# The last 512 tokens of x turned by VectorE and carried by sixteen transfers, in a fused state-space and feed-forward kernel

## The chip, the cores and the metric

The kernel runs on one core of a Trainium2 chip. The metric is the device time of one execution in microseconds, as a median of several runs. The engines of a core are TensorE (PE, with its weight loads as PEld), VectorE (DVE), ScalarE (ACT), GpSimd (POOL) and SyncE (SP), which here only issues transfers.

## What is computed

One input x of 2048 tokens by 448 features goes two ways, and a gate for each token mixes the results.

```python
def _A_ref(x, Lambda_re, Lambda_im, B_re, B_im, C_re, C_im, log_dt, Dskip):
    ...
    Lam_bar = jnp.exp(dt * Lam)
    B_bar = ((Lam_bar - 1.0) / Lam)[:, None] * Bmat
    Bu = jnp.einsum("bld,pd->blp", x + 0j, B_bar)
    for t in range(L):
        h = Lam_bar[None, :] * h + Bu[:, t, :]
    ...
    y = 2.0 * jnp.einsum("blp,dp->bld", hseq, Cmat).real + x * Dskip[None, None, :]

def _B_ref(x, w1, w2):
    h = _silu(jnp.einsum("bsd,df->bsf", x, w1))
    return jnp.einsum("bsf,fd->bsd", h, w2)

g = _sigmoid((x * gate_w).sum(-1, keepdims=True))
return g * a + (1 - g) * b
```

The feed-forward width is 1792, the state has 448 complex channels, and everything that goes in or out is bf16.

## The kernel before

The 2048 tokens are cut into four chunks of 512 (`tc` 0 to 3). x is loaded with tokens in the partitions (`xnat`, `load_xn`, L423). The products need it with features in the partitions: `xT`, in four groups of 128 features that start at the columns `XCOL = [0, 128, 256, 320]`, the last two overlapping. For chunks 1 to 3 `x_transposes` (L498) has PE make 32 transposes of 64 by 64 against an identity (L508) into two PSUM banks, and two engines empty these into xT (L516 on DVE, L518 on ACT); for chunk 3 both evictions are ACT's.

`x_products` (L647) multiplies xT by w1 (tiles named F, 14 a chunk, emptied by ACT with the silu into `aT`) and by the state's input weights BT (tiles named B, 7 a chunk, emptied into `UG`: by DVE for chunk 0, by ACT for the others, L640 and L642). Each tile is a sum over seven products of 64 rows (L663), two tiles at a time in two PSUM banks.

`lanes` (L703 to L766) is DVE's large part, chunk by chunk: it turns UG by a phase (products with COS and SIN) into H, runs seven scans over 512 tokens (`tensor_tensor_scan`, L736) into Gf, and turns the result back into H. For chunks 0 to 2 POOL's queue carries each scan from Gf back to UG, cast to bf16 (L390 by way of L744); for chunk 3 ACT copies it. A chunk's scans start from the end of the chunk before (`gin`).

`ffn2` (G, L774) multiplies aT by w2. ACT empties it into one of two buffers `fe` (L780), scaled by the gate, and POOL's queue adds fe to xnat by an accumulating transfer (L782); the buffer may be filled again when that transfer has landed. xnat then holds g times the skip term, written by ACT at L849. `readout` (C, L795) multiplies H by the output weights CP, DVE adds xnat (L798), and SP stores the rows (L801). `gates` (L833) makes the gate: DVE's products xg and xnat (L704), ACT's sums (L842) and the tanh. `readout_weights` makes CP from C, with DVE's evictions at L827 and L830.

`H[3]` first holds the input weights B as they were loaded (`Bnat`, L411), then serves as chunk 3's H from `lanes(3)` on.

The order of the work comes from a planner (`Plan.order`, L104). PE takes its work in the order in which it was written; for the other engines the planner picks, at each point, the ready operation with the smallest priority number, by estimated durations and hops. PSUM banks are given out in the same pass. `Waits` (L204) then writes the engines' lists, with a semaphore wait wherever an operand is made or read elsewhere. So an added operation moves others on its engine, and the built program fixes the result. Loads by SP go first in its list; behind them it has only the stores.

Of the kernel before, what the change touches and what calls it, by code (L numbers as in the profile page):

```python
# [11 lines left out]
BF16 = DT.bfloat16  # L12
I32 = DT.int32

S_TOK = 2048
D_MOD = 448
F_FF = 1792
CH = 512
# [4 lines left out]
NOT = 5  # L23
NWARM = 6
NFILL = 2
XCOL = [0, 128, 256, 320]

TURN = 6.283184
# [248 lines left out]
def bass_gated_mix__ssm_conv_s5__dense_activation_silu__prompt_kernel(nc, A_x, A_Lambda_re, A_Lambda_im, A_B_re, A_B_im, A_C_re, A_C_im,  # L277
               A_log_dt, A_Dskip, B_x, B_w1, B_w2, gate_w, out):
    with ExitStack() as ctx:
# [6 lines left out]
        x2, out2 = A_x[0], out[0]  # L286

        xnat = sb("xnat", [128, NTB, D_MOD], BF16)
        xT = sb("xT", [128, 4, S_TOK], BF16)
        w1s = sb("w1s", [128, 4, F_FF], BF16)  # L290
        w2s = sb("w2s", [128, NFB, D_MOD], BF16)
        BT = sb("BT", [128, 4, 896], BF16)
# [175 lines left out]
        def x0_transposes(q0, part, who):  # L468

            tk = Ps(2)  # L470

            def mm(pe):
                for q in (q0, q0 + 1):
                    for k in range(2):
                        o = ((q - q0) * 2 + k) * 64
                        for h in range(2):
                            p = slice(64 * h, 64 * h + 64)
                            r = pe.transpose(bk(tk, h).bitcast(BF16)[:, o:o + 64], xnat[p, 2 * part + k, XCOL[q]:XCOL[q] + 128], ident[p, p])  # L478
                return r
            PE(mm, [f"xn0{part}", "ident"], [tk], 4 * 0.054, "xT0")  # L480
            for h in range(2):
                src = lambda h=h: bk(tk, h).bitcast(BF16)[:, 0:256].rearrange("p (q b n) -> p q b n", q=2, n=64)
                dst = xT[:, q0:q0 + 2, 256 * part:256 * part + 256].rearrange("p q (b h n) -> p q b h n", h=2, n=64)[:, :, :, h, :]
                names = [f"xT0_{q}{part}{h}" for q in (q0, q0 + 1)]
                if who[h] == "d":
                    DVE(lambda e, src=src, dst=dst: e.tensor_copy(dst, src()), [tk], names, 0.28, 0, "xTe")  # L486
                else:
                    ACT(lambda e, src=src, dst=dst: e.activation(dst, src(), AF.Copy), [tk], names, act_cost(256), 0, "xTe")
# [4 lines left out]
        x0_transposes(2, 1, "dd")  # L493

        xn_of = {tc: {q: [f"xT{tc}_{h}" for h in range(2)] for q in range(4)} for tc in range(1, NCH)}
        xn_of[0] = {q: [f"xT0_{q}{part}{h}" for part in range(2) for h in range(2)] for q in range(4)}

        def x_transposes(tc, who):  # L498

            tk = Ps(2)  # L500

            def mm(pe):
                for q in range(4):
                    for b in range(4):
                        o = (q * 4 + b) * 64
                        for h in range(2):
                            p = slice(64 * h, 64 * h + 64)
                            r = pe.transpose(bk(tk, h).bitcast(BF16)[:, o:o + 64],  # L508
                                             xnat[p, 4 * tc + b, XCOL[q]:XCOL[q] + 128], ident[p, p])
                return r  # L510
            PE(mm, [f"xn{tc}", "ident"], [tk], 16 * 0.035, f"xT{tc}")
            for h in range(2):
                src = lambda h=h: bk(tk, h).bitcast(BF16).rearrange("p (q b n) -> p q b n", q=4, b=4)
                dst = xT[:, :, tc * CH:(tc + 1) * CH].rearrange("p q (b h n) -> p q b h n", h=2, n=64)[:, :, :, h, :]
                if who[h] == "d":
                    DVE(lambda e, src=src, dst=dst: e.tensor_copy(dst, src()), [tk], [f"xT{tc}_{h}"], 0.69, 2.2, "xTe")  # L516
                else:
                    ACT(lambda e, src=src, dst=dst: e.activation(dst, src(), AF.Copy), [tk], [f"xT{tc}_{h}"], act_cost(1024), 2.2, "xTe")  # L518

        cosn = [f"COS{k}" for k in range(4)] + ["COSd"]  # L520
        sinn = [f"SIN{k}" for k in range(4)] + ["SINd"]
# [101 lines left out]
        def evict(pair, tk):  # L623

            kinds = [t[0] for t in pair]
            for k, n in ((0, 2),) if pair[0][:2] == pair[-1][:2] and len(pair) == 2 else ((0, 1), (1, 1))[:len(pair)]:
                kind, tc, a = pair[k]
                step = pair[k + 1][2] - a if n == 2 else 1
                sl = slice(a, a + step * (n - 1) + 1, step)
                names = [t[2] for t in pair[k:k + n]]  # L630
                src = (lambda: bk2(tk)) if n == 2 else (lambda k=k: bk(tk, k)[:, None, :])
                if kind == "F":
                    dst = aT[tc % 2][:, sl, :]
                    ACT(lambda e, src=src, dst=dst: e.activation(dst, src(), AF.Silu),  # L634
                        [tk, "tbl"], [f"aT{tc % 2}_{m}" for m in names], act_cost(512 * n), 2.5, "silu")
                    continue
                U, un = UG[tc % 2], f"U{tc % 2}_"
                dst = U[:, sl, :]
                if tc == 0:
                    DVE(lambda e, src=src, dst=dst: e.tensor_copy(dst, src()), [tk], [f"{un}{m}" for m in names], 0.15 + 0.53 * n, 2.6, "U")  # L640
                else:
                    ACT(lambda e, src=src, dst=dst: e.activation(dst, src(), AF.Copy), [tk], [f"{un}{m}" for m in names], act_cost(512 * n), 5, "U")  # L642
                if 3 in names:
                    load("pool", U[0:64, 7, :], U[64:128, 3, :], un + "7a", 65536, 9, [un + "3"])
                    load("pool", U[64:128, 7, :], U[0:64, 3, :], un + "7b", 65536, 9, [un + "3"])

        def x_products(tiles, fill={}, wait=()):  # L647

            part = (list(zip([(i, 64) for i in (0, 1, 2, 3)], [(i, 0) for i in (0, 1, 3, 2)])),
                    list(zip([(i, 0) for i in (0, 1, 2)], [(i, 64) for i in (0, 1, 3)])))
            pairs = [tiles[t:t + 2] for t in range(0, len(tiles), 2)]
            toks = [Ps(2) for _ in pairs]

            def steps(k, h, a, z):
                def body(pe):
                    for n, cut in list(enumerate(part[h]))[a:z]:  # L660
                        for b, ((i, p0), tile) in enumerate(zip(cut, pairs[k])):
                            tc = tile[1]
                            r = pe.matmul(bk(toks[k], b), weights(tile, p0, p0 + 64, i), xT[p0:p0 + 64, i, tc * CH:(tc + 1) * CH],  # L663
                                          start=(h == 0 and n == 0), stop=(h == 1 and n == 2))
                    return r
                reads = [n for cut in part[h][a:z] for (i, _), tile in zip(cut, pairs[k])
                         for n in xn_of[tile[1]][i] + (w1n(tile[2], i) if tile[0] == "F" else btn[tile[2]])]
                return PE(body, list(dict.fromkeys(reads)), [toks[k]], (z - a) * PE_MM[512], f"{pairs[k][0][0]}{pairs[k][0][1]}")

            def half(k, h):  # L670
                if h == 0 and pairs[k][0] == ("F", 0, 0):
                    def zero(pe):
                        for n in range(NFILL):
                            for b, p in enumerate((slice(64, 128), slice(0, 64))):
                                r = pe.matmul(bk(toks[k], b)[:, 0:128], ones[p, 0:128], ones[p, 0:128], start=True, stop=True)  # L675
                        return r
                    PE(zero, [], [toks[k]], NFILL * 0.11, "fill")
                    steps(k, 0, 0, 2)
                    steps(k, 0, 2, 4)
                else:  # L680
                    steps(k, h, 0, len(part[h])).own = h == 1
                if h:
                    evict(pairs[k], toks[k])

            half(0, 0)
            for f in fill.get(-1, ()):
                f()
            for k in range(len(pairs)):
                order = [lambda: half(k, 1)] + [lambda: half(k + 1, 0)] * (k + 1 < len(pairs))
                for n, f in enumerate(order if k - 1 in wait else order[::-1]):  # L690
                    f()
                    for m in fill.get((k, n), ()):
                        m()
                for f in fill.get(k, ()):
                    f()
# [173 lines left out]
        gates(0)  # L869
        gates(1)  # L870
        lanes(1)
        for f in cp(0) + G(0, 1) + cp(1, 2) + G(2, 3) + cp(3):
            f()
        x_products(F(1) + F(2, 0, 1) + B(2), {2: xt(2, "aa")})
        gates(2)
        lanes(2)
        for f in G(4, 5, 6, 7) + C(0, 1, 2, 3):
            f()
        x_products(F(2, 1) + B(3) + F(3), {1: xt(3, "aa"), 9: [lambda: gates(3), lambda: lanes(3)]})
        for f in C(4, 5, 6, 7) + G(8, 9, 10, 11):  # L880
            f()
        for f in C(8, 9, 10, 11) + G(12, 13, 14, 15) + C(12, 13, 14, 15):
# [36 lines left out]
```

## Time and profile before

| what | us |
|---|---|
| median of three runs | 141.94 |
| lowest and highest of them | 141.46, 142.53 |
| the profiled execution | 141.25 |
| its span, first to last instruction | 139.5 |
| busy in it: PE | 135.9 |
| DVE | 122.0 |
| ACT | 90.3 |
| POOL | 39.2 |
| chunk 3's transposes on PE (32, at 77.23) | 0.47 |
| chunk 3's evictions of xT on ACT (2, at 78.19) | 1.93 |

Times in the views are microseconds from the start of the span. The chain of work that ended last is followed back from the last instruction: at each step to what released it, or to the instruction before it on its engine. A timeline line gives start, length, engine, source line, operation, what is written from what, shapes, and in brackets the idle time before it with what ended it; neighbours of the same kind are merged (x2). For transfers, the time to landing runs from the issue to the semaphore.

### The profile page before, as it was taken

What the parts mean: (1) busy time and instruction counts of PE and PEld (TensorE: products, weight loads), DVE (VectorE), ACT (ScalarE), POOL (GpSimd) and SP (SyncE); (2) the same over time, 40 slices, a digit from 0 to 9 for tenths busy, and PEclk for the clock granted to TensorE, in tenths of its full rate; (3) what the DMA queues carried; (4) which work ended last, traced back from release to release, by engine and by line L of the source; (5) the groups of instructions that cost most, each with busy time, mean ns of one, the idle gap of its engine ahead of it and who ended that gap; (6) DMA issues with size and microseconds to landing.
All of it is one profiled execution on the core that took longest, in us unless ns stands there. A gap on an engine that the chain in (4) does not pass through costs nothing.

```text
span 139.5 us, 3000 instructions
## 1 busy us (share of the span) xinstructions
PE 135.9 (97%) x1201; PEld 67.0 (48%) x1201; DVE 122.0 (87%) x179; ACT 90.3 (65%) x157; POOL 39.2 (28%) x72
## 2 busy tenths in 40 slices
PE   7999999999999999999999999999999999999992
PEld 2445454455544544455544544444455555555561
DVE  0319999999999999999999999999999999997053
ACT  3349768999989999823694887799931268312300
POOL 7134040100248440227733001824000314022220
PEclk9999999999999999999999999999999999999999
DMA  4998999510156770104976200674202322323242
GB/s 136 337 294 243 363 320 238 177 42 0 31 79 94 129 110 1 38 15 73 157 131 155 38 5 0 95 133 79 38 4 97 66 33 36 83 83 61 40 94 71
DMA packets 17956, 14.71 MB, mean 105 GB/s; under 512 B 2835, under 2 KB 17814, under 8 KB 17942
## 3 DMA queue, kind: packets, MB, share of 16 engines
q0 software_dynamic: 6064, 5.51, 24.8%
q1 hardware_dynamic: 11318, 8.65, 20.7%
q10 hardware_dynamic: 560, 0.36, 0.8%
q8 instruction: 9, 0.15, 0.4%
q14 instruction: 5, 0.04, 0.1%
HBM read 7.17 MB, written 1.84 MB: 65 GB/s over the span
## 4 chain that ended last, share of the span: by engine, by line
PE 97%; DVE 0%; issue 0%
PE ps L663 46%; PE ps L774 31%; PE ps L795 15%; PE ps L463 2%; PE ps L508 1%; PE ps L478 1%; PE ps L814 1%; PE ps L604 1%; DVE ot L798 0%; PE ps L675 0%; PE ps L464 0%; PE ps L536 0%
## 5 line engine op out<-in xcount | busy, mean ns | idle before, releaser
L663 PE MATMUL ps<-xT,w1s 64*128 64x512 bf16 x392 | 48.5, 378 | 0.0
L774 PE MATMUL ps<-w2s,aT 128*128 128x448 bf16 x224 | 43.2, 353 | 0.0
L634 ACT ACTIVATE aT<-ps 128x1024 bf16<-128x1024 f32 (+1 forms) x30 | 28.7, 969 | 8.5 <-PE ps L663 8.4
L774 PEld LDWEIGHTS ps<-w2s,aT 128*128 128x128 bf16 x224 | 21.7, 98 | 20.4 <-ACT xnat L849 0.4
L663 PEld LDWEIGHTS ps<-xT,w1s 64*128 64x128 bf16 x392 | 19.7, 94 | 22.3 <-DVE xT L486 0.7
L663 PE MATMUL ps<-xT,BT 64*128 64x512 bf16 x196 | 25.8, 376 | 0.0
L782 POOL DMA_DIRECT2D xnat<-fe x16 | 14.1, 900 | 37.9 <-ACT fe L780 37.2
L780 ACT ACTIVATE fe<-ps,g 128x448 bf16<-128x448 f32 x16 | 10.1, 632 | 21.1 <-PE ps L774 21.0
L390 POOL DMA_DIRECT2D UG<-Gf x27 | 14.7, 549 | 20.9 <-DVE Gf L736 20.4
L736 DVE TENSOR_TENSOR_SCAN Gf<-rc,gin,H 128x512 f32<-128x512 f32 x14 | 17.2, 1268 | 0.0
L795 PE MATMUL ps<-CP,H 128*128 128x448 bf16 (+2 forms) x98 | 16.4, 326 | 0.0
L663 PEld LDWEIGHTS ps<-xT,BT 64*128 64x128 bf16 x196 | 10.8, 94 | 11.1 <-DVE Gf L562 0.2
L798 DVE SCALAR_TENSOR_TENSOR ot<-ps,g,xnat 128x448 bf16<-128x448 f32 (+2 forms) x18 | 10.8, 622 | 6.0 <-issue 4.6
L390 POOL DMA_DIRECT2D UG<-UG x8 | 4.8, 597 | 29.2 <-ACT UG L642 17.4
L704 DVE TENSOR_TENSOR H<-UG,COS 128x3584 bf16<-128x3584 bf16 (+4 forms) x10 | 12.6, 1266 | 0.0
L795 PEld LDWEIGHTS ps<-CP,H 128*128 128x128 bf16 x98 | 8.9, 98 | 7.5 <-DVE k L752 0.4
L642 ACT ACTIVATE UG<-ps 128x1024 bf16<-128x1024 f32 (+1 forms) x12 | 10.7, 923 | 1.4 <-PE ps L663 1.4
L842 ACT ACTIVATE junk<-xg 128x448 bf16<-128x448 bf16 x16 | 9.2, 574 | 2.1 <-DVE xg L704 2.0
L849 ACT ACTIVATE xnat<-xnat,g 128x448 bf16<-128x448 bf16 x16 | 9.8, 671 | 0.2
L704 DVE TENSOR_TENSOR PI<-UG,SIN 128x512 bf16<-128x512 bf16 (+2 forms) x13 | 9.1, 722 | 0.0
L704 DVE TENSOR_TENSOR PO<-UG,SIN 128x1536 bf16<-128x1536 bf16 (+1 forms) x8 | 8.7, 1087 | 0.1
L736 DVE TENSOR_TENSOR_SCAN Gf<-rc,gin,H2C 128x512 f32<-128x512 f32 x7 | 8.5, 1265 | 0.0
(102 smaller groups left out, 126.5 us busy)
## 6 DMA issues: line engine op xcount, KB each, us to landing
UG<-Gf POOLq DMA_DIRECT2D x21, 128.0 KB, 2.5
xnat<-fe POOLq DMA_DIRECT2D x16, 112.0 KB, 2.6
out_dram<-ot SPq DMA_DIRECT2D x15, 112.0 KB, 1.7
w2s<-in_B_w_dram SPq DMA_DIRECT2D x1, 1568.0 KB, 11.8
xnat<-in_A_x_dram SPq DMA_DIRECT2D x3, 448.0 KB, 6.1
w1s<-in_B_w_dram SPq DMA_DIRECT2D x1, 576.0 KB, 6.2
UG<-UG POOLq DMA_DIRECT2D x8, 64.0 KB, 2.2
H2C<-in_A_C_re_dram SPq DMA_DIRECT2D x2, 196.0 KB
```

The source lines that it names most:

```text
L390: P.add(q, lambda e: e.dma_start(dst, src), list(after), name.split(), 0.6 if q == "pool" else 0.5, prio, sem(), nbytes, tag="ld " + name)
L634: ACT(lambda e, src=src, dst=dst: e.activation(dst, src(), AF.Silu), [tk, "tbl"], [f"aT{tc % 2}_{m}" for m in names], act_cost(512 * n), 2 ...
L642: ACT(lambda e, src=src, dst=dst: e.activation(dst, src(), AF.Copy), [tk], [f"{un}{m}" for m in names], act_cost(512 * n), 5, "U")
L663: r = pe.matmul(bk(toks[k], b), weights(tile, p0, p0 + 64, i), xT[p0:p0 + 64, i, tc * CH:(tc + 1) * CH], start=(h == 0 and n == 0), stop=( ...
L704: DVE(lambda e: e.tensor_tensor(o, a, b, op), r, w, dve_cost(n, 2), prio, tag)
L736: DVE(lambda e, s=s, b=b, init=init: e.tensor_tensor_scan(Gf[:, s, :], rc[:, b:b + 1].to_broadcast([128, CH]), A[:, s, :], init, ALU.mult, ...
L774: r = pe.matmul(bk(tk)[:, 0:D_MOD], aT[tc % 2][:, fb, o:o + 128], w2s[:, fb, :], start=(fb == 0), stop=(fb == NFB - 1))
L780: ACT(lambda e: e.activation(f[:, :], bk(tk)[:, 0:D_MOD], AF.Copy, scale=g1[:, tb:tb + 1]), [tk, f"g1_{tc}"], [fn], act_cost(448, 1), 7, "fe")
L782: P.add("pool", lambda e: e.dma_start(Tb[:, tb, :], f[:, :], accum_op=ALU.add), [fn, f"Tb{tb}"], [f"Tb{tb}"], 0.94, 2, sem(), 115000, tag= ...
L795: r = pe.matmul(bk(tk)[:, 0:b - a], H[tc][:, s, o:o + 128], CP[:, s, a:b], start=(s == 0), stop=(s == NSLOT - 1))
L798: DVE(lambda e, tk=tk, a=a, b=b: e.scalar_tensor_tensor(ot[tb % NOT][:, a:b], bk(tk)[:, 0:b - a], g[:, tb:tb + 1], Tb[:, tb, a:b], ALU.mul ...
L849: ACT(lambda e, tb=tb: e.activation(Tb[:, tb, :], xnat[:, tb, :], AF.Copy, scale=g[:, tb:tb + 1]), [f"xd{tc}", f"g_{tc}"], [f"Tb{tb}"], ac ...
```

## The change

Chunk 3 no longer passes through PE. `x_blocks(3)`, written down between the first readout weights and `x_products` of chunk 1, turns x on DVE in blocks of 32 by 32: four instructions, of 768 and 256 elements a partition for two of the four token blocks each. They write into the first four slots of `H[3]`, which hold nothing between the making of BT and `lanes(3)`. A block that is turned lies in the partitions of its tokens' group, so sixteen transfers on SP's queue, one for each pair of a group of 32 tokens in a block (g) and a group of 32 features (m), carry it to its partitions in xT. Each has 32 partitions of 16 rows of 32 elements (64 bytes). They share one semaphore, and the products of chunk 3 wait for all of them. The four instructions have priority 15, ahead of `gates` (19) and `lanes` (20 and up).

xT is laid out by chunk. The eviction of chunk 0's B tiles goes to DVE where the pair's first index is in `UDVE`. Chunk 2 keeps its transposes.

```diff
+XPRIO = {3: 15}
+XBLK = (3,)
+UDVE = (0, 2, 4, 6)
...
-        xT = sb("xT", [128, 4, S_TOK], BF16)
+        xT = sb("xT", [128, NCH, 4, CH], BF16)
...
+        for tc in XBLK:
+            xn_of[tc] = {q: [f"xT{tc}_{g}{m}" for g in range(4) for m in range(4)] for q in range(4)}
...
+        def x_blocks(tc):
+            X32 = H[3][:, 0:4, :].rearrange("p m (q b i) -> p m q b i", q=4, i=32)
+            names = [f"H3_{s}" for s in range(7)] + ["H3_3i"]
+            xs = xnat[:, 4 * tc:4 * tc + 4, :]
+            for q0, q1, c in ((0, 3, 0), (3, 4, XCOL[3])):
+                n = q1 - q0
+                for b0, b1 in ((0, 2), (2, 4)):
+                    src = xs[:, b0:b1, c:c + 128 * n].rearrange("p b (q m i) -> p b q m i", q=n, i=32)
+                    dst = X32.rearrange("p m q b i -> p b q m i")[:, b0:b1, q0:q1, :, :]
+                    DVE(lambda e, dst=dst, src=src: e.transpose(dst, src), [f"xn{tc}"], names, 0.15 + 256 * n / 960, XPRIO[tc], "xTd")
+            k = sem()
+            for g in range(4):
+                for m in range(4):
+                    to = xT[32 * m:32 * m + 32, tc, :, :].rearrange("p q (b g i) -> p (q b) g i", b=4, i=32)[:, :, g, :]
+                    P.add("sp", lambda e, to=to, g=g, m=m: e.dma_start(to, X32[32 * g:32 * g + 32, m, :, :, :].rearrange("p q b i -> p (q b) i")),
+                          names, [f"xT{tc}_{g}{m}"], 0.5, 400, k, 32768, tag="xTm")
...
-                if tc == 0:
+                if tc == 0 and a in UDVE:
...
+        if 3 in XBLK:
+            x_blocks(3)
+        x_products(F(1) + F(2, 0, 1) + B(2), {2: xt(2, "aa")} if 2 not in XBLK else {})
...
-        x_products(F(2, 1) + B(3) + F(3), {1: xt(3, "aa"), 9: [lambda: gates(3), lambda: lanes(3)]})
+        x_products(F(2, 1) + B(3) + F(3), {1: xt(3, "aa") if 3 not in XBLK else [], 9: [lambda: gates(3), lambda: lanes(3)]})
```

More of the change, by code (lines that the diff above doesn't have):

```diff
@@ L482, in x0_transposes @@
                 src = lambda h=h: bk(tk, h).bitcast(BF16)[:, 0:256].rearrange("p (q b n) -> p q b n", q=2, n=64)
-                dst = xT[:, q0:q0 + 2, 256 * part:256 * part + 256].rearrange("p q (b h n) -> p q b h n", h=2, n=64)[:, :, :, h, :]
+                dst = xT[:, 0, q0:q0 + 2, 256 * part:256 * part + 256].rearrange("p q (b h n) -> p q b h n", h=2, n=64)[:, :, :, h, :]
                 names = [f"xT0_{q}{part}{h}" for q in (q0, q0 + 1)]
@@ L513, in x_transposes @@
                 src = lambda h=h: bk(tk, h).bitcast(BF16).rearrange("p (q b n) -> p q b n", q=4, b=4)
-                dst = xT[:, :, tc * CH:(tc + 1) * CH].rearrange("p q (b h n) -> p q b h n", h=2, n=64)[:, :, :, h, :]
+                dst = xT[:, tc, :, :].rearrange("p q (b h n) -> p q b h n", h=2, n=64)[:, :, :, h, :]
                 if who[h] == "d":
@@ L662, in body @@
                             tc = tile[1]
-                            r = pe.matmul(bk(toks[k], b), weights(tile, p0, p0 + 64, i), xT[p0:p0 + 64, i, tc * CH:(tc + 1) * CH],
+                            r = pe.matmul(bk(toks[k], b), weights(tile, p0, p0 + 64, i), xT[p0:p0 + 64, tc, i, :],
                                           start=(h == 0 and n == 0), stop=(h == 1 and n == 2))
@@ L871, in bass_gated_mix__ssm_conv_s5__dense_activation_silu__prompt_kernel @@
         lanes(1)
+        if 2 in XBLK:
+            x_blocks(2)
         for f in cp(0) + G(0, 1) + cp(1, 2) + G(2, 3) + cp(3):
             f()
-        x_products(F(1) + F(2, 0, 1) + B(2), {2: xt(2, "aa")})
+        if 3 in XBLK:
+            x_blocks(3)
+        x_products(F(1) + F(2, 0, 1) + B(2), {2: xt(2, "aa")} if 2 not in XBLK else {})
         gates(2)
```

## The prediction

> **What bounds the kernel now.** I read the page's busy shares first, then its chain that ended last, then the same chain in order of time, and last the timelines of the engines that the change loads or relieves.
>
> ```profile
> PE 135.9 (97%) x1201; PEld 67.0 (48%) x1201; DVE 122.0 (87%) x179; ACT 90.3 (65%) x157; POOL 39.2 (28%) x72
> PE 97%; DVE 0%; issue 0%
> ```
>
> The first line is busy time, share and instructions of each engine, the second the shares of the chain. TensorE (PE) has no hole that another engine could be blamed for: whatever leaves PE's list shortens the time, as long as nobody makes PE wait instead. From the chain in order of time (start, length, what; us):
>
> ```profile
> 77.23 0.47 PE ps L508 x32
> 77.70 21.80 PE ps L663 x202
> ...
> 120.79 10.59 PE ps L774 x56
> 131.38 5.35 PE ps L795 x42
> ```
>
> The first line is what the change removes, the last the read-out of the last 512 tokens, which needs all of H3 from VectorE (DVE). DVE's timeline (start, length, engine, line, operation, tiles, forms; idle time in brackets) at its two ends of interest:
>
> ```profile
> 27.43 0.16 DVE L569 TENSOR_TENSOR sc1s<-scc,SG 128x8 f32<-128x8 f32 x1
> 27.51 0.68 DVE L704 TENSOR_TENSOR H<-UG,COS 128x1024 bf16<-128x1024 bf16 x1
> ...
> 126.07 2.09 DVE L704 TENSOR_TENSOR H<-H,PO 128x2048 bf16<-128x2048 bf16 x2
> 132.80 0.69 DVE L798 SCALAR_TENSOR_TENSOR ot<-ps,g,xnat 128x448 bf16<-128x448 f32 x1 [4.64 <-issue]
> ```
>
> The table by stretches gives DVE 100.28 us busy in the 100.70 from 27.50 to 128.20. So DVE has no air: work added at 27.5 delays everything behind it, up to the last subtraction into H3 (end 126.07 + 2.09 = 128.16). The 4.64 us of idle time behind that are the only reserve.
>
> **What is removed.** 32 transposes on PE: 0.47 us of the chain, from the line above; no work hides them, so the full 0.47 is gained. Two evictions on ScalarE (ACT), 1.93 us at 78.19: ACT waits 2.08, 0.49 and 0.31 us for PE around them, so their going gains nothing. The split of tokens 0 to 511's evictions by `UDVE` changes nothing: B(0)'s pairs start at 0, 2, 4 and 6, all in the list. xT's new layout leaves each matmul a contiguous row of 512: zero.
>
> **What DVE gets: four 32 by 32 transposes of 768, 768, 256 and 256 elements a partition.** No row shows this operation. Start to start, bf16 products take 0.335 us for 512 elements and 1.00 for 1792: 0.52 ns an element and 0.07 an instruction, together 1.34 us, the lower bound. Operations at one element a step (f32 subtraction of 512: 0.60; cast of 1024 from PSUM: 1.13) give 1.04 ns and 0.07: 2.41 us. The scan (512 in 1.13) gives 2.07 ns: 4.5 us, the upper bound. I take 2.41: one source, one result and no recurrence is nearest to the middle row.
>
> **What it waits for.** In the new order the first transpose stands right ahead of the product at 27.51, and it needs x's last load. That is issued at 21.8 and took 6.1 us to land, so 27.9: DVE waits 0.4 us (0 to 0.5, since the queue moves nothing after 28). DVE's lag is then 0.4 + 2.4 = 2.8 us. Its evictions of the CP weights are put further forward: the first pair comes at 27.9 + 2 x 0.87 + 0.60 + 0.34 = 30.6 (before 30.39), the second at 36.3 (36.33), so PSUM banks come free as before. The product xg of tokens 512 to 1023 comes at 42.1 instead of 38.68, and ACT's sums with it; the gate made of them is first needed by ACT's L780 at 60.03, against 50.39 now. The lag meets PE at four read-outs: 67.94 (H0 ready 57.84), 99.50 (86.17), 115.49 (106.18), 131.38 (128.16). The first three have 9 us or more; the last has 3.22, or 2.87 to its first weight load at 131.03, and 0.47 less once PE is earlier: 2.40 to 2.75. Lag less reserve: 0.05 to 0.4 us of stall, of which DVE's 0.42 us of idle time may swallow part; I take 0.2. With the bounds on the transposes the stall runs from 0 to 2.5.
>
> **What SyncE and its queue get: sixteen transfers.** SP issues two loads in 1.65 and 0.44 each earlier, so about 0.5 us apiece, 8 us from 32.7 on. SP has nothing to do from 22.95 to the first store at 70.30; that hole hides the issues, and nothing is queued behind the first one's wait for DVE. Each transfer moves 32 x 16 rows of 64 bytes: 8192 packets in all, on 16 DMA engines. Three answers bound a packet (queue, packets, MB, share of 16 engines): the tail from 137.2 to 139.5, the stretch 20 to 22, and the page's row of POOL's queue:
>
> ```profile
> q1 hardware_dynamic: 504, 0.17, 27.9%
> ...
> q1 hardware_dynamic: 773, 0.39, 94.7%
> ...
> q0 software_dynamic: 6064, 5.51, 24.8%
> ```
>
> 0.279 x 16 x 2.3 / 504 = 20 ns (mean 340 bytes), 39 ns, and 91 ns (rows that are cast or accumulated). That makes 10, 20 or 47 us. I take 20 ns, the smallest packets seen: transfers from 33 to about 45. xT's last quarter is first read at 81.9, now 81.4. At 47 us, and with POOL's own traffic in between, that would fail; otherwise it is covered.
>
> **Who shares the DMA engines then.** Between 33 and 45 the DMA engines carry POOL's accumulating transfers of fe into xnat. ACT may not refill its two fe buffers before they land. ACT and POOL show how close that is:
>
> ```profile
> 40.88 1.34 ACT L780 ACTIVATE fe<-ps,g 128x448 bf16<-128x448 f32 x2
> 42.12 0.57 ACT L842 ACTIVATE junk<-xg 128x448 bf16<-128x448 bf16 x1
> ...
> 37.99 1.79 POOL L782 DMA_DIRECT2D xnat<-fe  x2 [0.71 <-ACT xnat L849]
> ```
>
> The refills end at 42.22; they free the two banks that PE's third pair takes after 22 matmuls of 0.108 us from 40.15, at 42.53. So PE has 0.2 to 0.3 us to spare, and every later landing of the first two transfers comes out of PE. In the new order the first scan's UG<-Gf, at 36.70 now, falls behind these two on POOL, which helps them; PE waits for nothing there today, so the lower bound is still nothing. The upper is what POOL's UG copies met when the SP queue was full (issue to landing; stretch 18 to 20, then 26 to 28):
>
> ```profile
> UG<-UG POOLq DMA_DIRECT2D x2, 64.0 KB, 6.4
> ...
> UG<-UG POOLq DMA_DIRECT2D x2, 64.0 KB, 2.8
> ```
>
> That is 3.6 us more, a stall of up to 3.4. Between them: 128 packets of 91 ns over 16 engines are 0.73 us a transfer; sharing the engines evenly doubles that, less the slack, and something for the second behind the first. I take 0.6 us, nearer to the lower end, because SP's issues leave the queue about as busy as it can drain (0.65 us of packets every 0.5 us) where the full queue of 18 to 20 had a backlog of large rows.
>
> At this place a rule of the Trainium skill speaks against the change. DMA: Bandwidth & Descriptors, section Specifications, puts the least size for full rate at 512 bytes and says that smaller transfers are read, modified and written. By that each packet would cost two passes, 41 ns, the transfers would run to 54, and the stall would be nearer 3.4 than 0.6 (by that rule, about 144.9): the rival of the queue below, whose chance holds it. The rows from 137.2 to 139.5, of under 512 bytes, go to HBM and show 20 ns; no run here shows 64-byte writes into SBUF.
>
> **Sum.** -0.47 + 0.6 = +0.1; a stall at 42 moves PE's last read-out back too, so the 0.2 at the end vanishes in it. The profiled execution took 141.25 (span 139.5, 1.75 around it); it is 0.69 under the median of the runs. Its sum is 141.4, and the median's 142.1. That is the forecast. No change can be told from one under 1% (1.4 us) here; the three runs span 1.07.
>
> **The rivals.**
> - All is hidden: packets drain faster than they are issued, DVE's lag is within 2.4. Then 141.94 - 0.47 = 141.5. For it: the reserve of 2.40 to 2.75 is about the lag. Against: ACT's refill has 0.2 us.
> - Slower, by the queue: the accumulating transfers land up to 3.6 us late, at 38 to 42. It decides from 1.9 us of PE stall on, and ends at up to 141.94 - 0.47 + 3.4 = 144.9. For it: the 6.4 us above. Against: that backlog was of large rows.
> - DVE becomes the bound at the end: transposes at the scan's rate, lag 4.9, stall 4.9 - 2.6 = 2.3, time 143.8. Against: a scan feeds each result into the next.
> - xT's last quarter comes late: 91 ns a packet, 47 us from 33, and 10 us of POOL's traffic between (45.6% of 36 to 45, 58% of 45 to 55): 90, so PE waits 8 us: 150. Against: those rows are cast or accumulated.
>
> **How the numbers follow.** Forecast, a stall of 0.2 to 1.9 us: 0.38. All hidden: 0.21. The queue: 0.24. DVE at the end: 0.09. Late xT: 0.05. Faster by over 1% would need 1.4 us where 0.47 are removed: 0.03, for what I overlook. Within 1% are the first two, 0.59; slower are the next three, 0.38. The range runs from 141.2 (all hidden, less the profile's scatter) to 145.2 (the queue's upper end and as much), and leaves out late xT and half of the 0.03; the forecast's own range is 141.6 to 143.4.
>
> **What would show it.** Right: no L508 in the chain at 77; four transposes of 0.9 and 0.35 us from 27.9; the last H3 subtraction near 131; fe's refill later than 42.2, and a PE hole of about half a us behind it. Wrong: transposes of twice that; a hole ahead of the last L795; SP transfers still moving past 60; no hole in PE at all.

## The result, and the profile after

| | before | after |
|---|---|---|
| median, us (9 runs each) | 141.69 | 143.25 |
| lowest and highest | 141.45, 142.53 | 142.58, 148.03 |
| profiled execution; its span | 141.25; 139.5 | 142.58; 140.8 |
| first matmul of the last read-out on PE | 131.22 | 132.51 |

The ratio is 1.0091, with a 95% interval from 1.0063 to 1.0118: 1.3 us slower (0.9 to 1.7), so within the 1% that the forecast called the same, though the interval reaches beyond it. The ratio leaves out executions that ran over 1.5% above the fastest of their kernel (three of the nine here, 146.1 to 148.0, which do stand in the median), and where the profiled execution of an experiment was such a one, marked *order only*, only who waits for whom is read from it.

Line numbers: the lines from L640 on stand 24 further down in the changed kernel (L663 is L687, L774 is L798, L795 is L819), L508 is L513 and L390 is L393; the transposes are L536 and the sixteen transfers L541. First the page's busy shares and its chain of the changed kernel, to be laid beside those of before:

```profile
PE 135.5 (96%) x1169; PEld 66.2 (47%) x1169; DVE 124.5 (88%) x183; ACT 89.3 (63%) x155; POOL 38.9 (28%) x72
PE 81%; DVE 11%; DMA 3%; issue 1%; ACTq 1%; ACT 0%; DVEq 0%
```

PE does 0.4 us less and DVE 2.5 us more, as the change says. The new thing is in the second line: 11% of the chain that ended last now runs through DVE, where PE had 97% and DVE none; the 3% of DMA is a load of w1 at the very start. The same chain in order of time shows where (start, length, what; us):

```profile
40.23 0.89 PE ps L687 x7
...
43.52 1.09 DVE xg L728
...
45.95 6.71 DVE Gf L760 x6
...
56.24 1.96 DVE H L728
...
58.28 0.61 ACT UG L666
...
58.93 10.77 PE ps L798 x56
69.70 5.29 PE ps L819 x28
75.00 25.79 PE ps L687 x238
...
132.67 5.36 PE ps L819 x42
```

PE is 0.08 us behind its old place at 40.23 (40.15 before). Then the chain leaves PE for DVE until 58.2, passes through one of ACT's evictions, and is back on PE at 58.93 with G(4), which began at 57.24 before: PE is 1.69 us behind, nearly all of it lost in this one stretch. The removed transposes (L508 at 77.23) are no longer there and 0.47 come back; from there to the end the distance stays at 1.29. (The chain counts a piece on PE from the end of the piece before it, so its last one begins 0.16 us after the first matmul of the table.) The chain enters DVE only at 41; what made DVE late before that has to be read from DVE's own timeline. PE's timeline has the two holes of that stretch (start, length, engine, line, operation, tiles; in brackets the idle time before it and what ended it):

```profile
43.09 3.20 PE L687 MATMUL ps<-xT,w1s 64*128 64x512 bf16 x28 [0.49 <-ACT fe L804]
...
58.93 2.25 PE L798 MATMUL ps<-w2s,aT 128*128 128x448 bf16 x11 [0.95 <-ACT UG L666]
```

The first was forecast, the second was not. ACT's timeline tells what ACT itself waited for in the two places:

```profile
42.40 0.64 ACT L804 ACTIVATE fe<-ps,g 128x448 bf16<-128x448 f32 x1 [0.77 <-DMA xnat<-fe]
...
58.28 0.60 ACT L666 ACTIVATE UG<-ps 128x512 bf16<-128x512 f32 x1 [0.84 <-DVE H L728]
```

At 42.40 it is the second accumulating transfer of fe, which landed 3.63 us after its issue, where it took 2.94 before. At 58.28 it is DVE: chunk 2's B tiles go into the buffer of UG that chunk 0 used (`tc % 2`), and DVE's product H<-UG,COS still had to read it. PE's G(4) needs the PSUM banks that this eviction empties. DVE's timeline has the cause and the other end:

```profile
29.39 0.98 DVE L536 STREAM_TRANSPOSE H<-xnat 128x768 bf16<-128x768 bf16 x1 [1.71 <-DMA xnat<-in_A_x_dram]
...
33.24 0.43 DVE L536 STREAM_TRANSPOSE H<-xnat 128x256 bf16<-128x256 bf16 x1
...
56.16 2.03 DVE L728 TENSOR_TENSOR H<-UG,COS 128x3584 bf16<-128x3584 bf16 x1
...
130.35 2.10 DVE L728 TENSOR_TENSOR H<-H,PO 128x2048 bf16<-128x2048 bf16 x2
134.10 0.69 DVE L822 SCALAR_TENSOR_TENSOR ot<-ps,g,xnat 128x448 bf16<-128x448 f32 x1 [1.65 <-issue]
```

DVE waits 1.71 us for x's last load (issued at 22.75, landed at 29.35), and the transposes take 0.90, 0.89, 0.36 and 0.36 start to start, 2.51 us; it had been 0.08 late before. Together that is, to 0.01 us, the lag of 4.29 us which it shows from here on. The reading product ends at 58.19 where it ended at 53.90, and the last subtraction into H3 at 132.45 where it ended at 128.16: the lag is carried whole to the end. The idle time behind it fell from 4.64 to 1.65 us, and PE's first read-out matmul begins at 132.51, right on the subtraction. How much DVE could be late at 58 is seen in before, in DVE's and in ACT's timeline:

```profile
51.89 2.02 DVE L704 TENSOR_TENSOR H<-UG,COS 128x3584 bf16<-128x3584 bf16 x1
```

```profile
54.32 0.59 ACT L642 ACTIVATE UG<-ps 128x512 bf16<-128x512 f32 x1
```

After the change G(4) begins 0.74 us behind the end of that product (58.93 against 58.19); before, the product ended at 53.90 and G(4) came at 57.24. So DVE had 57.24 - 53.90 - 0.74 = 2.6 us to spare here, no more than at the last read-out.

The transfers did nothing late. SP's timeline, and the DMA queue's row of the stretch from 36 to 39 (queue, packets, MB, share of 16 engines):

```profile
34.36 12.22 SPq L541 DMA_DIRECT2D xT<-H  x16
```

```profile
q1 hardware_dynamic: 2299, 0.14, 42.0%
```

SP takes 0.76 us for each. The last is issued near 46 and lands near 48; the products first read it at 83.4. A packet of 61 bytes in the mean takes 0.42 x 16 x 3 / 2299 = 8.8 ns.

### The profile page after: what moved, and what is told of

Read it like the earlier page. It is cut to its first block, busy times and chain, and to the rows that moved or that the text cites. A ratio compares the mean times of both kernels' runs of the same rounds, so it can differ in the third digit from the quotient of the medians.

```text
span 140.8 us, 2954 instructions
## 1 busy us (share of the span) xinstructions
PE 135.5 (96%) x1169; PEld 66.2 (47%) x1169; DVE 124.5 (88%) x183; ACT 89.3 (63%) x155; POOL 38.9 (28%) x72
## 4 chain that ended last, share of the span: by engine, by line
PE 81%; DVE 11%; DMA 3%; issue 1%; ACTq 1%; ACT 0%; DVEq 0%
PE ps L687 34%; PE ps L798 30%; PE ps L819 15%; DVE Gf L760 6%; DVE H L728 3%; DMA w1s<-in_B_w_dram 3%; DVE xg L728 1%; PE ps L838 1%; DVE xnat L728 1%; ACTq L393 1%; PE ps L628 1%; ACT UG L666 0%; PE ps L513 0%; DVE k L776 0%; DVE ot L822 0%
## 5 line engine op out<-in xcount | busy, mean ns | idle before, releaser
L687 PE MATMUL ps<-xT,w1s 64*128 64x512 bf16 x392 | 48.2, 376 | 0.8 <-ACT fe L804 0.5
L798 PE MATMUL ps<-w2s,aT 128*128 128x448 bf16 x224 | 43.2, 353 | 1.0 <-ACT UG L666 1.0
L798 PEld LDWEIGHTS ps<-w2s,aT 128*128 128x128 bf16 x224 | 21.7, 98 | 21.4 <-ACT UG L666 1.4
L687 PEld LDWEIGHTS ps<-xT,w1s 64*128 64x128 bf16 x392 | 19.7, 94 | 23.4 <-ACT fe L804 1.0
L687 PE MATMUL ps<-xT,BT 64*128 64x512 bf16 x196 | 25.8, 376 | 0.0
L393 POOL DMA_DIRECT2D UG<-Gf x27 | 14.6, 566 | 19.8 <-DVE Gf L760 19.6
L819 PE MATMUL ps<-CP,H 128*128 128x448 bf16 (+2 forms) x98 | 16.4, 326 | 0.0
L687 PEld LDWEIGHTS ps<-xT,BT 64*128 64x128 bf16 x196 | 10.8, 94 | 11.0 <-DVE Gf L586 0.2
L819 PEld LDWEIGHTS ps<-CP,H 128*128 128x128 bf16 x98 | 8.8, 98 | 7.6 <-DVE Gf L760 0.4
L393 POOL DMA_DIRECT2D UG<-UG x8 | 4.7, 594 | 26.6 <-ACT UG L666 14.4
L873 ACT ACTIVATE xnat<-xnat,g 128x448 bf16<-128x448 bf16 x16 | 9.4, 665 | 0.2
L770 ACT ACTIVATE UG<-Gf 128x512 bf16<-128x512 f32 (+1 forms) x9 | 5.6, 628 | 5.8 <-DVE Gf L760 5.7
```

What stands on the lines that cost most here:

```text
L393: P.add(q, lambda e: e.dma_start(dst, src), list(after), name.split(), 0.6 if q == "pool" else 0.5, prio, sem(), nbytes, tag="ld " + name)
L798: r = pe.matmul(bk(tk)[:, 0:D_MOD], aT[tc % 2][:, fb, o:o + 128], w2s[:, fb, :], start=(fb == 0), stop=(fb == NFB - 1))
L819: r = pe.matmul(bk(tk)[:, 0:b - a], H[tc][:, s, o:o + 128], CP[:, s, a:b], start=(s == 0), stop=(s == NSLOT - 1))
L873: ACT(lambda e, tb=tb: e.activation(Tb[:, tb, :], xnat[:, tb, :], AF.Copy, scale=g[:, tb:tb + 1]), [f"xd{tc}", f"g_{tc}"], [f"Tb{tb}"], ac ...
```

## The experiments

Three theories. **A**: DVE's lag is what costs; it is paid where chunk 2's eviction waits for UG, and again without extra cost at the last read-out, and PE pays the larger of that and the hole at 42. **B**: the hole at 42, from the transfers' share of the DMA engines, is the whole cost. **C**: the two add. Each run of five rounds stands beside before on the same chip. Intervals are of 95%.

**Each half alone.** The transposes without the transfers; PE and ACT turn chunk 3 as before:

```diff
-            k = sem()
-            for g in range(4):
-                for m in range(4):
...
-        x_products(F(2, 1) + B(3) + F(3), {1: xt(3, "aa") if 3 not in XBLK else [], ...
+        x_products(F(2, 1) + B(3) + F(3), {1: xt(3, "aa"), ...
```

> The four transposes stay on DVE at their place, but their result is not used: no transfers, and PE and ACT transpose chunk 3 as before (extra work, nothing left out). Theory A: DVE's lag and the hole at 58 stay, PE's 0.47 us come back: 143.3 to 143.6 (1.011 to 1.014). Theory B: without the transfers nothing is lost: 141.7 to 142.0 (1.000 to 1.002).

And the transfers without the transposes; they carry rows of x as they are, so that chunk 3 is computed from x that is not turned:

```diff
-                    DVE(lambda e, dst=dst, src=src: e.transpose(dst, src), ...
...
-                          names, [f"xT{tc}_{g}{m}"], 0.5, 400, k, 32768, tag="xTm")
+                          [f"xn{tc}", "CP4"], [f"xT{tc}_{g}{m}"], 0.5, 400, k, 32768, tag="xTm")
```

> The sixteen transfers without the DVE transposes: they carry rows of x as they lie, issued once the first CP weights are made (about 31), with the same 8192 rows of 64 bytes. Chunk 3's xT then holds x that is not transposed. Theory A: DVE has no lag, no hole at 58; only the hole at 42 (up to 0.5) is left against the 0.47 saved: 141.2 to 141.8 (0.997 to 1.001). Theory B: the whole loss stays: 142.8 to 143 (1.008 to 1.009).

Measured: transposes alone 1.0064 (1.0034 to 1.0095), transfers alone 1.0018 (0.9994 to 1.0043). For the transposes alone both numbers are missed, A's 1.011 to 1.014 as well as B's 1.000 to 1.002; for the transfers alone A's is met. PE's and DVE's timelines of the first:

```profile
57.70 1.50 PE L790 MATMUL ps<-w2s,aT 128*128 128x448 bf16 x7 [0.47 <-ACT UG L658]
```

```profile
28.17 0.98 DVE L534 STREAM_TRANSPOSE H<-xnat 128x768 bf16<-128x768 bf16 x1 [0.58 <-DMA xnat<-in_A_x_dram]
```

With no transfer in the queue there is no hole at 42, and the hole at 58 is there: 0.47 us at a lag of 0.58 + 2.47 = 3.05, where 3.05 - 2.6 = 0.45 was to be expected. B falls: it asked for no cost. This execution took 141.77 us, among the shorter ones (141.63 to 143.61), so its lag need not be the usual one. The transfers alone keep the gain of 0.47 and end 0.26 above before, so they cost 0.73 us (0.38 to 1.08). ACT's timeline (order only) has it waiting for the landing of fe, and nobody waits at 58:

```profile
44.45 0.64 ACT L804 ACTIVATE fe<-ps,g 128x448 bf16<-128x448 f32 x1 [2.48 <-DMA xnat<-fe]
```

By the times, C is the nearer one: the two runs are 0.91 and 0.26 us above before, which makes 1.17 where 1.29 was measured. A has PE pay the larger of 0.91 and 0.73 and keep the 0.47, which makes 0.44. The order of waiting inside one execution speaks for A, the times of the halves for C, and the further runs do not settle it.

**The wait for x's load.** Two ways: load chunk 3 of x ahead of chunk 2,

```diff
+        load_xn(3)
         load_xn(2)
-        load_xn(3)
```

> Only the order of x's last two loads is swapped, so that the last 512 tokens are issued first. Theory A (DVE's lag): DVE waited 1.7 us for this load and was 4.3 us late from there on; the lag is paid at 58, where ACT may not empty chunk 2's tiles into chunk 0's UG buffer before DVE has read it for the last time, as PE shift = lag - 2.6. With the load 0.7 to 1.2 us earlier the time falls by about as much: 142.0 (ratio to the kernel before 1.001 to 1.004). Theory B (the shared DMA queues: the 64-byte transfers delay fe's landing, and that hole of PE at 42 is the loss): nothing changes, 143.0 (1.009).

and transposes that read blocks of w2, which have long landed, so that chunk 3 is computed from other data (the priority is set so that they stand at almost the same place of DVE's list, 26.7):

```diff
-XPRIO = {3: 15}
+XPRIO = {3: 19.5}
...
-            xs = xnat[:, 4 * tc:4 * tc + 4, :]
+            xs = w2s[:, 0:4, :]
...
-                    DVE(lambda e, dst=dst, src=src: e.transpose(dst, src), [f"xn{tc}"], names, ...
+                    DVE(lambda e, dst=dst, src=src: e.transpose(dst, src), ["w2"], names, ...
```

> The four transposes turn four blocks of w2, which has landed by 22, instead of x's last tokens, at almost the same place in DVE's list (XPRIO 19.5), and the transfers carry the result: chunk 3 is computed from other data, all else is alike. It takes the wait for the load away and nothing else. Theory A (two causes: DVE's lag of wait and transposes, and fe's late landing; PE pays the larger of the two): lag 2.6 us, under the slack at 58, so only the hole at 42 of 0.5 to 0.8 is left: 141.6 to 142.1 (1.000 to 1.003). Theory B (the queue alone): 142.8 to 143 (1.008 to 1.009). Theory C (both add up): 142.2 to 142.6 (1.004 to 1.007).

Measured: 1.0054 (1.0035 to 1.0073), the first matmul of the last read-out at 132.38, and 1.0034 (1.0005 to 1.0062), at 131.88. The first lies between A's number and B's, the second between A's and C's; B is missed twice. Without the wait the hole at 58 is gone. The one at 42 is left, and PE waits 0.19 us for H3 ahead of the last read-out. PE's timeline of the second run, and a line of its waits (total, count, longest):

```profile
43.14 3.19 PE L687 MATMUL ps<-xT,w1s 64*128 64x512 bf16 x28 [0.36 <-ACT fe L804]
```

```profile
PE ps L819 <- DVE H L728: 0.2, 1, 0.2
```

So the wait is a real part of the cost: 1.0091 to 1.0034 is 0.8 us, though the intervals only just part. The swap of the loads left 0.61 us of the wait and found a new one of 0.84 us, before the reading product at 56.03, for a UG<-Gf transfer that took 4.1 us to land (the same one took 3.2 in the profile after).

**Taking the meeting place away.** A third buffer of UG for chunk 2, on the room of `ct`:

```diff
-        UG = [sb(f"UG{k}", [128, 8, CH], BF16) for k in range(2)]
+        UG = [sb(f"UG{k}", [128, 8, CH], BF16) for k in range(3)]
...
-                U, un = UG[tc % 2], f"U{tc % 2}_"
+                U, un = UG[tc % 3], f"U{tc % 3}_"
```

> A third UG buffer for chunk 2 (the readout weights' work buffers lie in it until then), so that ACT need not wait for DVE's last reads of chunk 0 at 58. Theory A: the hole at 58 goes, the lag of 4 us then meets the read-out of chunk 3 at the end, whose reserve is 2.4 to 2.75, and the hole is there: 142.6 to 143.1 (1.007 to 1.010), nothing won. Rival: the shared buffer is the place where the time is lost for good; without it the time is that of the hole at 42 alone, 141.6 to 142.1 (1.000 to 1.003).

Measured: 1.0117 (1.0067 to 1.0166), from three executions alone. PE's waits (order only; total, count, longest):

```profile
PE ps L687 <- ACT fe L804: 1.6, 1, 1.6
...
PE ps L819 <- DVE H L728: 0.4, 1, 0.4
```

The wait at 58 is gone, as meant, and the time is not: PE comes earlier to the last read-out and waits there for H3. This is evidence for the second half of A: two places hold PE to the same lag, and opening one leaves the other. The w2 run, where the place at 58 was free too, shows the same order with its 0.19.

**Taking the hole at 42 away.** A third fe buffer:

```diff
-        fe = [sb(f"fe{k}", [128, D_MOD], BF16) for k in range(2)]
+        fe = [sb(f"fe{k}", [128, D_MOD], BF16) for k in range(3)]
...
-            f = fe[tb % 2]
+            f = fe[tb % 3]
```

> The changed kernel with a third fe buffer, so that ACT's third refill does not wait for an accumulating transfer to land. Theory A (VectorE's lag is paid at 58 us, where chunk 2's UG evictions wait for chunk 0's products, and PE pays the larger of that hole and the one at 42): the hole of 0.49 us at 43 goes, the one at 58 grows from 0.95 to about 1.4, G(4) still begins near 58.9, and the time stays 1.007 to 1.010 of before. Theory C (the two holes add): 1.004 to 1.006. Theory B (the queue's hole is the whole cost): 0.997 to 1.000.

Measured: 1.0054 (1.0029 to 1.008), the first matmul of the last read-out at 131.95. It did not do what it was meant to, so it judges neither A nor C. ACT's and DVE's timelines:

```profile
42.49 0.64 ACT L804 ACTIVATE fe<-ps,g 128x448 bf16<-128x448 f32 x1 [1.55 <-DMA xnat<-fe]
```

```profile
27.78 0.98 DVE L536 STREAM_TRANSPOSE H<-xnat 128x768 bf16<-128x768 bf16 x1
...
102.70 0.96 DVE L728 TENSOR_TENSOR PO<-UG,SIN 128x1536 bf16<-128x1536 bf16 x1 [0.96 <-DMA UG<-Gf]
```

The third refill came at 37.3, but ahead of ACT's writes of xnat (L873), which the accumulating transfers wait for; these left at 38.79 instead of 38.07, and the fourth refill waited for them just the same: PE's hole is 0.59. DVE's side tells more. The loads stand in the same order as in the changed kernel, and this time x's last load was issued at 21.80 and DVE hardly waited: the wait of 1.71 is one execution's. The lag at 56 is 2.65 and there is no hole at 58. But at 102.70 DVE waits 0.96 for a UG<-Gf, and the lag at the end is 3.74. The run with w2's blocks has the same wait there (0.90); the changed kernel has none.

Three fe buffers and the load of chunk 3 two places earlier, ahead of C's:

```diff
+        load_xn(3)
         load_C()
...
-        load_xn(3)
```

> Three fe buffers, and x's last load issued two places earlier on SP (ahead of C's), so that VectorE does not wait for it; its lag is then the four transposes alone, about 2.5 us, equal to the slack of 2.5 to 2.6 at 58. Theory A: no hole at 42, at most 0.2 at 58, and 0.997 to 1.000 of before (0.47 us saved, less up to 0.4 at the last read-out, whose reserve of 2.4 the lag just uses up). Theory B expects the same. Against both would be a hole of over 0.5 us at 58 with no wait of VectorE for the load: then the lag grows somewhere else.

Measured: 1.0037 (1.0007 to 1.0067). DVE does not wait for x, and the hole at 42 is gone, but A's number is missed. DVE's timeline (order only; everything starts some 3 us later here):

```profile
58.24 2.02 DVE L728 TENSOR_TENSOR H<-UG,COS 128x3584 bf16<-128x3584 bf16 x1 [0.93 <-DMA UG<-Gf]
```

That is the case the expectation held against both theories: a hole ahead of G(4) (0.61 us here) with no wait for the load. Part of the lag is made elsewhere, by DVE's wait for UG<-Gf, and the sixteen transfers had long landed when that UG<-Gf was issued.

**The transfers later.** They also wait for `Tb3`, the landing of fe's fourth transfer into chunk 0's rows of xnat, so that none runs at 42:

```diff
-                          names, [f"xT{tc}_{g}{m}"], 0.5, 400, k, 32768, tag="xTm")
+                          names + ["Tb3"], [f"xT{tc}_{g}{m}"], 0.5, 400, k, 32768, tag="xTm")
```

> The transposes stay at their place, the transfers also wait until fe's four transfers of chunk 0 have landed (about 46), so they run to about 58. Theory A: the hole at 42 goes, the lag and the hole at 58 stay and grow by as much: 142.6 to 143.1 (1.007 to 1.010), as the changed kernel. Theory B: the loss goes: 141.3 to 141.7 (0.997 to 1.000). Theory C: 142.2 to 142.5 (1.004 to 1.006). Kernel e3, without any transfers and with PE's 0.47 us put back, took 1.0064.

Measured: 1.0131 (1.0101 to 1.0161), the slowest of all and above every theory's number. No hole is left at 42, and the transfers are issued from 50 to 62, beside the scans' UG<-Gf (DVE's timeline, order only):

```profile
59.85 2.03 DVE L728 TENSOR_TENSOR H<-UG,COS 128x3584 bf16<-128x3584 bf16 x1 [0.80 <-DMA UG<-Gf]
```

The hole at 42 comes from the transfers, then, for it goes with them. Whether this wait of DVE does is not shown: the run with the loads swapped and the one with the load two places earlier wait at the same product, the first for 0.84 us, with no transfer of x left in the queue. What makes this kernel the slowest was not found.

**The transposes later.** Priority 20.5 puts them behind chunk 0's scans, among the big products:

```diff
-XPRIO = {3: 15}
+XPRIO = {3: 20.5}
```

> XPRIO 20.5 instead of 15: the four transposes stand behind chunk 0's scans, near 50 to 58, the transfers run from about 60 to 72. Theory A: no wait for the load, a lag of 2.5 us that the slack of 2.6 at 58 and of 2.4 to 2.75 at the end just holds; no hole at 58, 141.2 to 141.6 (0.997 to 1.000). Theory B: the transfers now meet fe's transfers of chunk 1 at 61 to 72, the hole moves there and stays: 142.5 to 143 (1.006 to 1.009).

> The same kernel as the one with priority 20.5 and two fe buffers, again, beside the others on the same chip, to see whether its 0.9983 of before holds: theory A 0.997 to 1.000. Its profile is to show 0.47 us of PE's transposes gone and 0.2 to 0.4 us of PE idle ahead of the last read-out.

Measured: 0.9983 (0.9957 to 1.0009), and again 0.9988 (0.9957 to 1.002). DVE's timeline of the second run:

```profile
49.04 0.95 DVE L536 STREAM_TRANSPOSE H<-xnat 128x768 bf16<-128x768 bf16 x1
...
129.59 2.09 DVE L728 TENSOR_TENSOR H<-H,PO 128x2048 bf16<-128x2048 bf16 x2
```

A's number is met twice, B's 1.006 to 1.009 is missed. Nothing waits for x any more, PE has no hole at 42 or 58, and the transfers are issued from 58 to 69 and landed by 73.4. What is left is the end: the last subtraction ends at 131.68 and PE's read-out begins at 131.75, after 0.1 us of idle time (0.3 in the first run). The 0.47 us are gained and partly given back; no difference from before can be told. The edit takes away the wait for the load and the meeting with fe's transfers at once, so it does not part A from C.

With three fe buffers as well (both edits above):

> The transposes later in VectorE's list (priority 20.5, so that they stand at 49 to 58 us behind chunk 0's first products), and three fe buffers. Theory A: the products that free UG are no longer delayed, no hole at 42 or at 58, only some 0.3 us ahead of the last read-out: 0.997 to 0.999 of before, as with two buffers (0.9983), since the transfers then run from 58 to 69 where no fe buffer is short. Theory B: 0.996 to 0.998. A difference between this and two buffers of over 0.003 would mean that fe's landings matter in that place too.

Measured: 1.0012 (0.9981 to 1.0043). No gain: the difference from two buffers stays under the 0.003 that the expectation asked for. And with two of the four evictions of chunk 0's B tiles taken from DVE, to give it air at the end:

```diff
-XPRIO = {3: 15}
+XPRIO = {3: 20.5}
...
-UDVE = (0, 2, 4, 6)
+UDVE = (0, 2,)
```

> A version meant to be faster than both: the transposes behind chunk 0's scans as in e2, and UDVE (0, 2) instead of (0, 2, 4, 6), which takes 1.7 us of chunk 0's evictions (1.13 + 0.60) from DVE to ACT. Theory A: DVE's lag falls to about 1 us, the end's reserve holds it, PE keeps the 0.47 us: 141.0 to 141.4 (0.995 to 0.998). Rival: ACT, dense from 20 to 36, holds PE there by up to a microsecond: 141.7 to 142.4 (1.000 to 1.005).

Measured: 1.0005 (0.9982 to 1.0027). In its profile (order only) the last subtraction again ends well ahead of the read-out, so the air is there; but PE now waits for DVE in chunk 0, near 24. The time is the rival's, its reason (ACT holding PE) is not what this profile shows. No version beats before.

## Why the prediction was right, and which step was wrong

The forecast was 142.1 us and no difference above 1%; it is 1.3 us slower, inside the range and inside the 1%. That the time fell inside is in part luck. The forecast was -0.47 + 0.6, with the stall paid at 42; in the profiled execution it was -0.47 + 1.76, and PE lost the 1.76 to DVE's lag. Point by point:

- **PE's transposes, -0.47: right.** The piece is gone from the chain at 77, and the distance to before falls from 1.76 (69.70 against 67.94) to 1.29 (100.79 against 99.50).
- **The transposes on DVE, 2.41 us: nearly right.** 2.51, and 2.47 as the lag less the wait in the run without transfers. The middle row was the right one to take.
- **The hole at 42, 0.6 us: right in place, cause and size.** 0.49 in the profile after; 0.73 (0.38 to 1.08) as the whole cost of the transfers alone. In the profiled execution it is not what sets the time, because the lag that is paid at 58 is larger.
- **The packets, 20 ns: too much.** They took 8.8 ns. The rule of the Trainium skill that was weighed (DMA: Bandwidth & Descriptors, section Specifications: below 512 bytes a transfer is read, modified and written) would have had 41 ns as the prediction priced it; these packets of 61 bytes took less than the 20 ns that it would have doubled. **SP's issues, 0.5 us each: too little**, 0.76. They err in opposite directions; the transfers were done near 48 instead of 45, which costs nothing.
- **The wait for the load, "0.4 us (0 to 0.5, since the queue moves nothing after 28)": the step that failed.** It was 1.71 in the profiled execution: the load was issued 1 us later than in before and took 6.6 us instead of 6.1. With the lag as it was, 4.29, the prediction's own subtraction gives the result: 4.29 less the reserve of 2.40 to 2.75 is 1.54 to 1.89, and 1.07 to 1.42 with the 0.47; measured is 1.29. So in this execution the rival "DVE becomes the bound at the end" had the path right and its condition, transposes at the scan's rate, wrong. The sum "a stall at 42 moves PE's last read-out back too, so the 0.2 at the end vanishes in it" has the right form, the larger of the two, and took the wrong one for the larger. The bound was one execution's landing time, taken for the kernel's: in eight profiled executions with the loads in this order, x's last load landed between 27.6 and 29.4. With the transposes early the wait was 0.58 without the transfers and next to none with a third fe buffer, and 0.61 with the loads swapped.
- **"The lag meets PE at four read-outs": incomplete.** It meets PE first at 58, through a buffer: chunk 2's eviction reuses chunk 0's UG. The slack there, 2.6, is no larger than at the end, and so it changed where the time was lost, not how much: with the third UG buffer the loss came back at the end. Of the prediction's own signs, the refill (42.40), the hole of about half a us and the vanished L508 came; the last subtraction begins at 130.35 and ends at 132.45, later than its "near 131"; and of the signs of being wrong, a hole ahead of the last read-out is there in the w2 run and in the first with the transposes later (0.19 and 0.30), while after the change PE's first read-out matmul follows the subtraction by 0.06.

What stays open: the wait for the load explains the 4.29 of this execution, but not all of the mean. With next to no wait for the load, DVE picked up 0.9 to 1.0 us at 102 for a UG<-Gf that was issued in the same rhythm and landed later. One thing goes with it in the traces. The DMA queue named instruction moves single packets of 16 KB, and one of them begins while the UG<-Gf that DVE waits for is on its way, in all nine such waits of the profiles. The queue rows of the run with the loads swapped, from 50 to 52 (queue, packets, MB, share of 16 engines; then issue to landing):

```profile
q8 instruction: 1, 0.02, 5.2%
...
UG<-Gf POOLq DMA_DIRECT2D x3, 128.0 KB, 4.1
```

The packet takes 0.052 x 16 x 2 = 1.7 us. Two of the three transfers, issued at 50.80 and 51.91, take 4.1 us each, and DVE waits 0.84 for the second. At 102 the packet begins at 100.5 in the two runs that wait 0.90 and 0.96, and the transfer issued 2.1 us before it takes 4.2; in the run without transfers it begins at 97.2, and the transfers issued from then on take 2.2 to 2.3. The packet is also there without a wait: after the change it begins at 100.7, the transfer issued at 99.83 takes 3.1, and DVE comes later still. No experiment moved it, so it is a companion of the wait and not its shown cause.

And whether the costs of transposes and transfers only overlap (A) or in part add (C) is not settled. After the change, in both runs on the load and with the third fe buffer, the last read-out starts within 0.1 us of DVE's last subtraction, which speaks for A in each of these executions. But A's number was missed for the transposes alone and for the run without either cause of delay, and the times of the two halves add up better than they overlap.

## What to carry to other kernels

Work moved from a full engine to one that is 87% busy is not free because its last result has 3 us to spare: write down every place where its lag meets another engine, and among them the buffers that it must finish reading before others may refill them, and take the smallest reserve. An operation put early in a queue that never idles should depend only on data that landed long before; a landing time read from one execution is worth about 1 us either way here. And transfers that share the DMA engines are felt by whoever waits for a landing at that time, here by ACT's refill and through it by PE.

## What the runs showed of the hardware

- The 32 by 32 transpose of bf16 on DVE took 0.90 us start to start for 768 elements a partition and 0.36 for 256: 1.05 ns an element and 0.09 us an instruction, twice a bf16 product's 0.52 ns.
- 64-byte rows from SBUF to SBUF took 8.8 ns each on the DMA engines; the pace of sixteen transfers of 512 rows was SP's issue, 0.76 us each, with the engines 42% busy.
- Beside them an accumulating transfer of 112 KB landed in 3.63 us instead of 2.94.
- The queue named instruction moved packets of 16 KB; one took 1.7 us, and two transfers of 128 KB from SBUF to SBUF that were under way beside it took 4.1 us to land, where two issued 2 us earlier took 2.2. That the packet is the cause is not shown.
